# Modulation rows by blocks of 512 columns, with two tiles of x modulated ahead of the scale

## The chip, the cores and the metric

The kernel runs on one NeuronCore of a Trainium2 chip. The metric is the device time of one execution in microseconds, taken as the median of a few executions of the same program. Five engines work side by side, each through its own instructions in program order: TensorE (PE, matrix products into the eight PSUM banks of 128 x 512 words), VectorE (DVE), ScalarE (ACT), GpSimd (POOL) and SyncE (SP, which here only issues DMA). They wait for each other by semaphores.

## The reference, cut to what matters

One batch of 2048 rows (S) of 1024 columns (D). All six modulation rows come from one vector `c`.

```python
mod = (_silu(c) @ w_mod).reshape(c.shape[0], 6, 1, -1)
sa, ca, ga, sb, cb, gb = ...                       # six rows of 1024
h = _layernorm(x) * (1 + ca) + sa
x = x + ga * fourier(h)        # real part of a DFT along D, then along S, by products
h = _layernorm(x) * (1 + cb) + sb
x = x + gb * (gelu(h @ w1 + b1) @ w2 + b2)         # 1024 -> 3584 -> 1024
```

The change concerns the first line, for `sa` and `ca` (the first 2048 columns of `w_mod`, 8 MB), and the first use of them: `h` for the first two of the sixteen tiles of 128 rows of x.

## The kernel before, in words

Every large product is made in half precision from split operands. A value is written as a high half (an f16 copy, by ScalarE) and a low half (the rest, by VectorE), and each product is three passes: high by high, high by low, low by high. So every operand costs ScalarE one instruction and VectorE one before TensorE can use it.

The Fourier part comes first. `plain1` (its products are line 1121) makes the first block of 512 output columns of the DFT along S by sixteen operands n of 48 products each: n = 0 to 7 use the real half of the DFT matrix, and each brings in a new pair of tiles of x, k and k + 8; n = 8 to 15 use the imaginary half with the same x. `winograd1` (line 1171) makes the other three blocks with fewer products from combined quarters; `gemm2` (line 1403) is the DFT along D; `gemm3` and `gemm4` (lines 1597 and 1706) are the two layers of the MLP.

A tile of x passes through `x_tasks`. Its mean and square sum are made by ScalarE (lines 610 and 614, each with an accumulated sum) or, for the first pair, by VectorE's statistics (601, 603); a few VectorE steps on 128 x 2 values turn them into the factor of the row (623 to 627). Then VectorE subtracts the mean and multiplies by the row 1 + ca (642), multiplies by the factor and adds the row sa (643); ScalarE takes the high half (644), VectorE the low half (645), and `("h", k, n)` is ready. `split_c` (690, 693) does the same for the two halves of an operand of the DFT matrix, with 690 on ScalarE and 693 on VectorE.

The rows sa and ca must first be scaled by a power of two from their largest value, so that they fit f16. Before, the 8 MB come as eight loads of one k each (128 partitions x 2048 columns, 8 KB in one run); `mod_pe` sums k = 0, 3, 5 and 7 on TensorE in four banks with a copy of silu(c) as the left operand, in single precision (each such product of 512 columns is two passes in the trace); `mod_dve` sums k = 1, 2, 4 and 6 on VectorE in `macc`, one instruction over 2048 columns for each. Four products with ones (line 1474) add `macc` to the banks over the partitions, and `mod_rows` adds k = 7 (496), takes the maximum of each bank (516), makes the scale `sh` (517 to 520), modulates tile 0 in two halves (503, 508, 521, 526, 513), and writes the rows `sas` and `ca1s` out of PSUM for the other tiles (521, 527, 528). The second tile of the pair, tile 8, follows like every other.

The order of all work is written out when the program is built. The start, up to `mod_rows`, is written by hand; from there a planner holds a model clock for every engine (`clk`), a time at which each result is done (`done`), and streams of tasks with due times (`push`). Between the products of TensorE, `fill_to` emits the task that is due first among those that could start. `clk.update(...)`, `done["mod"]`, `done["h", 0, 0]` behind the hand-written part set the model's state, and `LANDS` how long a stored piece takes until it may be loaded again (`("st", "u")`: the pieces of the first DFT's result). Due times come from `T0 = 42.0` and 48 products of 0.2158 us for each n. So the hand-written part also settles the order that VectorE, ScalarE, GpSimd and SyncE have later.

Of the kernel before, what the change touches and what calls it, by code (L numbers as in the profile page):

```python
# [17 lines left out]
P = 128  # L18
# [17 lines left out]
def kernel(ctx, tc, x, cre, cim, dre, dim, w1, b1, w2, b2, c, wm, out):  # L36
# [180 lines left out]
    LANDS = {"dma": 2.0, "st": 4.0, ("st", "d"): 7.0, ("st", "u"): 5.0, ("st", "s"): 4.0, ("st", "z"): 4.0}  # L217
# [253 lines left out]
    def wm2(k):  # L471

        return at(O_U + 8 * k if k < 4 else O_H + 8 * (k - 4), 2048)

    def mbank(n):
        return banks8[:, 512 * n : 512 * n + 512]

    def mod_pe(k, first):

        for n in range(4):  # L480
            if first and n > 1:
                pe.matmul(mbank(n), ones[0:1, 0:P], ones[0:1, :], start=True, stop=False)
            pe.matmul(mbank(n), srep[:, k, :], wm2(k)[:, 512 * n : 512 * n + 512], start=first and n < 2, stop=False)

    def mod_dve(k, first):

        if first:
            dve.tensor_scalar(macc, wm2(k), scol[:, k : k + 1], None, op0=ALU.mult)
        else:
            dve.scalar_tensor_tensor(macc, wm2(k), scol[:, k : k + 1], macc, op0=ALU.mult, op1=ALU.add)  # L490

    def mod_rows(k, c_lo, x1):


        for n in (2, 3, 0, 1):
            pe.matmul(mbank(n), srep[:, k, :], wm2(k)[:, 512 * n : 512 * n + 512], start=False, stop=True)
        m, pm, sh, iu = (m1[:, j : j + 1] for j in range(4))
        (mv, cl), x_ = xs[0], xf(0)
        r, a = cl[:, 1, :], cl[:, 2, :]
        sl = [slice(512 * q, 512 * q + 512) for q in range(2)]  # L500

        def times_ca(q):
            dve.scalar_tensor_tensor(
                x_[:, sl[q]], x_[:, sl[q]], mv[:, 0, 0:1], mbank(2 + q), op0=ALU.subtract, op1=ALU.mult
            )

        def plus_sa(q):
            dve.scalar_tensor_tensor(
                x_[:, sl[q]], x_[:, sl[q]], r[:, 0:1], sas[:, sl[q]], op0=ALU.mult, op1=ALU.add
            )  # L510

        def lo(q):
            dve.tensor_tensor(hq[:, 3 * q, 0, 1], x_[:, sl[q]], hq[:, 3 * q, 0, 0], op=ALU.subtract)

        for j in (2, 3, 0, 1):
            dve.tensor_reduce(mx[:, j : j + 1], mbank(j), axis=AX.X, op=ALU.max, apply_absolute_value=True)
        dve.tensor_reduce(m, mx, axis=AX.X, op=ALU.max)
        pow2(pm, m)
        dve.reciprocal(sh, pm)
        dve.tensor_scalar(sh, sh, SH, None, op0=ALU.mult)  # L520
        act.activation(sas[:, sl[0]], mbank(0), AF.Copy, scale=sh)
        times_ca(0)
        dve.scalar_tensor_tensor(r, r, sh, a, op0=ALU.mult, op1=ALU.mult)
        plus_sa(0)
        x1.pop(0).run()
        act.activation(hq[:, 0, 0, 0], x_[:, sl[0]], AF.Copy)  # L526
        act.activation(sas[:, sl[1]], mbank(1), AF.Copy, scale=sh)
        act.activation(ca1s, banks8[:, 1024:2048], AF.Copy)
        x1.pop(0).run()
        c_lo.run()  # L530
        lo(0)
        times_ca(1)
        plus_sa(1)
        act.activation(hq[:, 3, 0, 0], x_[:, sl[1]], AF.Copy)
        x1.pop(0).run()
        lo(1)
        dve.tensor_scalar(iu, pm, 2.0**5 / SD, None, op0=ALU.mult)

# [49 lines left out]
    xst = [mk([P, 2, 12], F32, f"xst{n}") for n in range(2)]  # L588
    xs = [(mk([P, 2, 2], F32, f"xmv{n}"), mk([P, 4, 2], F32, f"xcl{n}")) for n in range(8)]

    def x_tasks(k):

        st, (mv, cl) = xst[k % 2], xs[k]
# [3 lines left out]
        if k < 1:  # L597
            for n, i in enumerate(tiles):
                sv = st[:, n].rearrange("p (h k) -> p h k", h=2)
                for h in range(2):  # L600
                    f = lambda sv=sv, h=h, i=i: dve.bn_stats(sv[:, h], xf(i)[:, 512 * h : 512 * h + 512])
                    t.append(Task("dve", 0.7, f, [("x", i)] + ([t[-1].key] if t else [])))
                t.append(Task("dve", 0.2, lambda sv=sv, n=n: dve.bn_aggr(mv[:, n], sv), [t[-1].key]))
            t += chain(("dve", 0.15, lambda: dve.tensor_scalar(ve, mv[:, :, 1], EPS, None, op0=ALU.add)))
            t[-1].deps = (t[-2].key,)
        else:

            junk = at(O_U, 1024, F16)
            for n, i in enumerate(tiles):
                f = lambda n=n, i=i: act.activation(junk, xf(i), AF.Copy, accum_out=mv[:, n, 0:1])  # L610
                t.append(Task("act", 1.35, f, [("x", i)]))
            t.append(Task("dve", 0.15, lambda: dve.tensor_scalar(ss, mv[:, :, 0], -1.0 / D, None, op0=ALU.mult), [t[-1].key]))
            for n, i in enumerate(tiles):
                f = lambda n=n, i=i: act.activation(junk, xf(i), AF.Square, bias=ss[:, n : n + 1], accum_out=mv[:, n, 1:2])
                t.append(Task("act", 1.35, f, [t[2].key]))

            def var():
                dve.tensor_scalar(ve, mv[:, :, 1], 1.0 / D, EPS, op0=ALU.mult, op1=ALU.add)

            t.append(Task("dve", 0.15, var, [t[-1].key]))  # L620
# [10 lines left out]
        if k == 0:  # L631
            s.pop()
        t += s
        root = t[-1].key
        for n, i in enumerate(tiles):
            if i == 0:
                continue
            x_, hv = xf(i), hq[:, 1:3, k] if n else hq[:, 0:4:3, k]
            x2 = x_.rearrange("p (q d) -> p q d", q=2)
            mean, op = (mv[:, n, 0:1], ALU.subtract) if k < 1 else (ss[:, n : n + 1], ALU.add)  # L640
            u = chain(
                ("dve", 1.3, lambda x_=x_, mean=mean, op=op: dve.scalar_tensor_tensor(x_, x_, mean, ca1s, op0=op, op1=ALU.mult)),  # L642
# [792 lines left out]
    def load_wm2(k):  # L1435
        sp.dma_start(wm2(k), wm[:, k, 0 : 2 * D])

# [16 lines left out]
    for k in range(7):  # L1454
        if k in (1, 2, 4, 6):
            mod_dve(k, k == 1)
        else:
            mod_pe(k, k == 0)
# [9 lines left out]
    done["x", 0] = done["x", 8] = 23.0  # L1468
    clk.update(dma=45.0, act=15.0, dve=22.0, pe=25.0)
    x0 = x_tasks(0)  # L1470
    for _ in range(12):
        x0.pop(0).run()
    for n in (2, 3, 0, 1):
        pe.matmul(mbank(n), ones[:, 0:P], macc[:, 512 * n : 512 * n + 512], start=False, stop=False)
# [519 lines left out]
```

## Time and profile before

| | |
|---|---|
| median of 3 runs | 1980.11 us (1979.96 to 1980.17) |
| profiled execution | 1977.33 us |
| its span, first to last instruction | 1975.6 us |
| mean granted TensorE clock | 0.997 |
| PE busy | 1950.2 us (99%) |
| DVE busy | 1426.9 us (72%) |
| ACT busy | 851.2 us (43%) |
| read and written in HBM | 263 MB and 138 MB |

How to read it. A line of the timeline gives the start, the time from start to end of the merged instructions, the engine, the line of the kernel, what is written and read with its shape, how many instructions were merged, and in brackets the idle time of the engine before it with what released it. A line of the windows gives a stretch, its length, the busy time and number of instructions of PE, the weight loads, DVE, ACT and POOL, then the granted TensorE clock (1.00 is full speed), the share of the DMA engines, and GB/s. A line of waits gives who waited, for whom, the sum, the number and the longest. PE's busy time counts a product from its start to its modelled end, and consecutive products overlap; their spacing is found from a run of them.

### The profile page before, as it was taken

The numbers are of one execution on the slowest core, as the hardware profiler recorded it, in microseconds if no ns is written. First come the engines' busy times: TensorE is split into PE (matmuls) and PEld (weight loads), VectorE is DVE, ScalarE is ACT, GpSimd is POOL, SyncE is SP. The second block draws the span as 40 slices with busy tenths as digits, with TensorE's granted clock in tenths as the row PEclk, the third lists the DMA queues.
The fourth block names the chain that finished last, engine by engine and source line by source line (L and its number), as shares of the span: only waits on it lengthen the run. The fifth ranks groups of instructions, "written<-read, shape, count | busy, mean of one in ns | idle before, by whom it ended". The sixth has DMA issues, their size and how long they took to land.

```text
span 1975.6 us, 23586 instructions
## 1 busy us (share of the span) xinstructions
PE 1950.2 (99%) x9004; PEld 887.3 (45%) x9004; DVE 1426.9 (72%) x1799; ACT 851.2 (43%) x1091; POOL 190.3 (10%) x282
## 2 busy tenths in 40 slices
PE   7999999999999999999999999999999999999999
PEld 2444444444444444444444444444444444444443
DVE  5977886898984477776689898989873453553566
ACT  4743432445542255554587456456323312312311
POOL 0012211221210012211020000000000000000000
PEclk9999999999999999999999999999999999999999
DMA  9248587688688867878866455344476432432324
GB/s 386 61 165 271 187 287 292 236 324 314 241 280 328 308 236 254 288 234 302 309 221 204 142 181 176 134 148 176 176 218 197 124 102 74 131 102 66 112 75 85
DMA packets 139362, 402.41 MB, mean 204 GB/s; under 512 B 15536, under 2 KB 15536, under 8 KB 134640
## 3 DMA queue, kind: packets, MB, share of 16 engines
q1 hardware_dynamic: 112528, 309.92, 46.6%
q0 software_dynamic: 26720, 90.98, 13.0%
q8 instruction: 70, 1.15, 0.2%
q14 instruction: 44, 0.36, 0.0%
HBM read 262.95 MB, written 137.89 MB: 203 GB/s over the span
## 4 chain that ended last, share of the span: by engine, by line
PE 84%; DVE 8%; DMA 4%; ACT 2%; issue 1%; SPq 0%; DVEq 0%; ACTq 0%
PE ps L1706 24%; PE ps L1597 24%; PE ps L1171 17%; PE ps L1403 14%; PE ps L1121 5%; DMA arena<-in_wm_dram 2%; DVE arena L693 1%; DMA arena<-s 1%; DVE arena L642 1%; DVE arena L407 1%; DVE arena L643 1%; DMA arena<-u 1%; PE ps L1305 1%; DVE arena L645 1%; DVE arena L553 1%
## 5 line engine op out<-in xcount | busy, mean ns | idle before, releaser
L1706 PE MATMUL ps<-arena 128*128 128x512 f16 x2352 | 511.2, 379 | 2.7 <-DMA arena<-w 1.1
L1597 PE MATMUL ps<-arena 128*128 128x512 f16 x2352 | 510.2, 379 | 0.0
L1171 PE MATMUL ps<-arena 128*128 128x512 f16 x2016 | 435.6, 379 | 1.8 <-DMA arena<-s 1.8
L1706 PEld LDWEIGHTS <-arena 128*128 128x128 f16 x2352 | 229.9, 98 | 281.8 <-issue 3.9
L1597 PEld LDWEIGHTS <-arena 128*128 128x128 f16 x2352 | 230.2, 98 | 276.8
L1752 DVE SCALAR_TENSOR_TENSOR arena<-ps,i4c,arena 128x1024 f32<-128x1024 f32 x179 | 229.3, 1281 | 145.2 <-PE ps L1706 143.1
L1171 PEld LDWEIGHTS <-arena 128*128 128x128 f16 x2016 | 197.1, 98 | 240.2 <-DMA arena<-s 2.8
L1403 PE MATMUL ps<-arena 128*128 128x512 f16 x1344 | 292.4, 379 | 0.9 <-DMA arena<-u 0.9
L395 ACT ACTIVATE arena<-arena,shc 128x512 f16<-128x512 f32 (+1 forms) x115 | 116.2, 1018 | 283.2 <-PE ps L1706 190.4
L1403 PEld LDWEIGHTS <-arena 128*128 128x128 f16 x1344 | 131.4, 98 | 157.1 <-DMA arena<-u 1.4
L1121 PE MATMUL ps<-arena 128*128 128x512 f16 x768 | 171.3, 386 | 7.0 <-ACT arena L526 3.9
L420 DVE TENSOR_TENSOR arena<-arena 128x512 f32<-128x512 f32 (+1 forms) x228 | 171.1, 753 | 4.2
L690 ACT ACTIVATE arena<-arena 128x1024 f16<-128x1024 f32 x100 | 104.1, 1050 | 146.9 <-PE ps L1171 113.1
L407 DVE SCALAR_TENSOR_TENSOR arena<-arena,shc 128x512 f16<-128x512 f32 (+1 forms) x115 | 128.5, 1121 | 35.8 <-ACT arena L395 35.4
L693 DVE SCALAR_TENSOR_TENSOR arena<-arena 128x1024 f16<-128x1024 f32 x100 | 128.6, 1303 | 18.6 <-ACT arena L690 18.6
L1623 DVE TENSOR_TENSOR arena<-arena,ps 128x512 f32<-128x512 f32 x84 | 57.6, 685 | 111.2 <-PE ps L1597 106.9
L1616 ACT ACTIVATE arena<-arena,b1s,i1c 128x512 f32<-128x512 f32 x84 | 68.3, 813 | 137.7 <-DVE arena L1623 137.7
L1121 PEld LDWEIGHTS <-arena 128*128 128x128 f16 x768 | 75.8, 99 | 102.8 <-issue 8.8
L782 ACT ACTIVATE arena<-arena 128x1024 f16<-128x1024 f32 x56 | 57.8, 1048 | 62.0 <-DMA u<-arena 21.4
L395 ACT ACTIVATE arena<-arena,s1c 128x512 f16<-128x512 f32 (+1 forms) x70 | 60.7, 884 | 41.3 <-DVE arena L420 30.1
L785 DVE TENSOR_TENSOR arena<-arena 128x1024 f16<-128x1024 f32 x56 | 66.9, 1218 | 15.0 <-ACT arena L782 15.0
L407 DVE SCALAR_TENSOR_TENSOR arena<-arena,s1c 128x512 f16<-128x512 f32 (+1 forms) x70 | 66.1, 959 | 10.8 <-ACT arena L395 10.7
(161 smaller groups left out, 1392.6 us busy)
## 6 DMA issues: line engine op xcount, KB each, us to landing
w<-arena SPq DMA_DIRECT2D x64, 512.0 KB, 4.3
arena<-w SPq DMA_DIRECT2D x119, 256.0 KB, 2.7
u<-arena POOLq DMA_DIRECT2D x56, 512.0 KB, 5.4
arena<-u SPq DMA_DIRECT2D x112, 256.0 KB, 4.2
arena<-w SPq DMA_DIRECT2D x56, 512.0 KB, 3.6
arena<-s SPq DMA_DIRECT2D x48, 512.0 KB, 7.7
arena<-in_cre_dram SPq DMA_DIRECT2D x32, 512.0 KB, 7.1
arena<-in_cim_dram SPq DMA_DIRECT2D x32, 512.0 KB, 5.6
```

Of the source, the lines that this page charges most:

```text
L395: act.activation(o[m][0], q(j), AF.Copy, **sc)
L407: dve.scalar_tensor_tensor(o[m][1], q(j), scale, o[m][0], op0=ALU.mult, op1=ALU.subtract)
L420: dve.tensor_tensor(q(d), q(a), q(b), op=op)
L690: h = Task("act", 1.15, lambda: act.activation(o[:, :, 0], s2, AF.Copy, scale=SC), list(deps) + free)
L693: dve.scalar_tensor_tensor(o[:, :, 1], s2, SC, o[:, :, 0], op0=ALU.mult, op1=ALU.subtract)
L1121: pe.matmul(bank_of(d_), hleft(d_, s, kp, a), cop(n)[:, s, b], start=(kp == 0 and s == 0 and a == 0 and b == 0), stop=(kp == 7 and s == 1 ...
L1171: pe.matmul(bank_of(st + ch), left, cop(n)[:, s, b], start=(start and kp == 0 and s == 0 and a == 0 and b == 0), stop=(kp == 3 and s == 1 ...
L1403: pe.matmul(bank_of(bk), up(N)[:, c_, a], dp(n)[:, c_, w], start=(start and ri == 0 and c_ == 0 and i == 0), stop=(ri == 1 and c_ == 3 and ...
L1597: pe.matmul(ps.rearrange("p (k t) -> p k t", k=4), w1c[:, m, s, a, d * P : (d + 1) * P], zc(m)[:, b, :, d, :], start=(start and d == 0 and ...
L1616: act.activation(dst, src, AF.Gelu_apprx_tanh, scale=inv, bias=b1s[:, 2 * p + j : 2 * p + j + 1])
L1706: pe.matmul(t[:, j], hidc[:, c_, m, a, k * P : (k + 1) * P], w2c[:, m, c_, w], start=(start and c_ == 0 and n == 0), stop=(c_ == 1 and n = ...
L1752: lambda: dve.scalar_tensor_tensor(dst, ps[b], inv, dst, op0=ALU.mult, op1=ALU.add), kp[b],
```

## The change

- The weights of the four half rows are loaded by column blocks of 512 in the order `MODS = (2, 0, 3, 1)`: first half of ca, first half of sa, second half of ca, second half of sa. A load has four k (128 x 4 x 512, runs of 2 KB); the last block's second load is cut into two of two k. Tiles 0 and 8 of x are loaded behind the first block.
- The sums lie in the last four banks instead of the first four. Within each block some k are summed by TensorE (`mod_pe`) and some by VectorE (`mod_dve`, now 512 columns at a time); `mod_sum` adds VectorE's part, `mod_top` takes the maximum of a bank as soon as it is complete.
- Tiles 0 and 8 get their mean and variance from ScalarE, and ScalarE makes `(x - mean) * factor` of both with one instruction each (`AF.Identity`). Tile 0's halves are multiplied by ca and sa is added straight from PSUM, and tile 8 is multiplied by ca, before the scale is known. With the scale, ScalarE's high half of tile 0 applies it in the same instruction, the low half likewise on VectorE; tile 8 takes one VectorE step with the scaled row `sas`. Tile 0 itself is multiplied by the scale at the end of the part.
- Tile 9's statistics move from ScalarE to VectorE.
- Fourteen products of a constant tile that nobody reads stand at the start of TensorE's order, and eight behind the last sum (`idle_pe`).
- The planner's starting state differs (`pe` 29.5 instead of 34.0, `("h", 0, 0)` 29.5 instead of 35.0, `("h", 0, 1)` given as 35.0, `mod` 33.5 instead of 33.0), and a stored u counts as landed after 7 instead of 5 us.

```diff
-    LANDS = {"dma": 2.0, "st": 4.0, ("st", "d"): 7.0, ("st", "u"): 5.0, ("st", "s"): 4.0, ("st", "z"): 4.0}
+    LANDS = {"dma": 2.0, "st": 4.0, ("st", "d"): 7.0, ("st", "u"): 7.0, ("st", "s"): 4.0, ("st", "z"): 4.0}
...
+    def load_wmb(n, k, w):
+        sp.dma_start(wmb(n, k, w), wm[:, k : k + w, 512 * n : 512 * n + 512])
+
+    def idle_pe(n):
+        w = ones.bitcast(F16)
+        for _ in range(n):
+            pe.matmul(banks8[:, 0:512], w[:, 0:P], w[:, 0:512], start=True, stop=True)
+
+    def mod_pe(n, k, first=False):
+        if first and n > 1:
+            pe.matmul(mbank(n), ones[0:1, 0:P], ones[0:1, :], start=True, stop=False)
+        pe.matmul(mbank(n), srep[:, k, :], wmb(n, k)[:, 0], start=first and n < 2, stop=False)
...
+    def mod_sum(n):
+        pe.matmul(mbank(n), ones[:, 0:P], acc_of(n), start=False, stop=True)
+
+    def mod_top(n):
+        dve.tensor_reduce(mx[:, n : n + 1], mbank(n), axis=AX.X, op=ALU.max, apply_absolute_value=True)
...
-    load_wm2(0)
-    for k in range(1, 7):
-        load_wm2(k)
-    for i in (0, 8):
-        load_x(i).run()
-    load_wm2(7)
+    for n in MODS:
+        for k, w in ((0, 4), (4, 4)) if n != 1 else ((0, 4), (4, 2), (6, 2)):
+            load_wmb(n, k, w)
+        if n == 2:
+            load_x(0).run()
+            load_x(8).run()
...
+    idle_pe(14)
+    part(2, (0, 1, 2, 3), 2, True)
+    part(2, (4, 5, 6, 7), 3)
+    steps("act", "act", "dve", "act", "act")
+    part(0, (0, 1, 2, 3), 2, True)
+    mod_sum(2)
+    steps("dve", "act")
+    part(0, (4, 5, 6, 7), 3)
+    steps("dve", "dve", "dve", "dve")
+    dve.tensor_tensor(r, r, a, op=ALU.mult)
+
+    dve.tensor_tensor(ss, ss, r, op=ALU.mult)
+    for n, v in enumerate((x_, y_)):
+        act.activation(v, v, AF.Identity, scale=r[:, n : n + 1], bias=ss[:, n : n + 1])
+    mod_top(2)
+    part(3, (0, 1, 2, 3), 2, True)
+    mod_sum(0)
+    dve.tensor_tensor(xh[0], xh[0], mbank(2), op=ALU.mult)
+    part(3, (4, 5, 6, 7), 3)
+    dve.tensor_tensor(xh[0], xh[0], mbank(0), op=ALU.add)
+    mod_top(0)
+    part(1, (0, 1, 2, 3), 2, True)
+    mod_sum(3)
+    mod_top(3)
+    part(1, (4, 5), 1)
+    dve.tensor_tensor(xh[1], xh[1], mbank(3), op=ALU.mult)
+    part(1, (6, 7), 1)
+    mod_sum(1)
+    idle_pe(8)
     c_hi, c_lo = c0[0][1]
     c_hi.run()
+    dve.tensor_tensor(y_, y_, both(2), op=ALU.mult)
+    mod_top(1)
+    dve.tensor_reduce(m, mx, axis=AX.X, op=ALU.max)
+    pow2(pm, m)
+    dve.reciprocal(sh, pm)
+    dve.tensor_scalar(sh, sh, SH, None, op0=ALU.mult)
+    act.activation(hq[:, 0, 0, 0], xh[0], AF.Copy, scale=sh)
+    dve.tensor_tensor(xh[1], xh[1], mbank(1), op=ALU.add)
+    act.activation(hq[:, 3, 0, 0], xh[1], AF.Copy, scale=sh)
+    dve.scalar_tensor_tensor(hq[:, 0, 0, 1], xh[0], sh, hq[:, 0, 0, 0], op0=ALU.mult, op1=ALU.subtract)
+    act.activation(sas, both(0), AF.Copy, scale=sh)
+    c_lo.run()
+    dve.scalar_tensor_tensor(hq[:, 3, 0, 1], xh[1], sh, hq[:, 3, 0, 0], op0=ALU.mult, op1=ALU.subtract)
+    act.activation(ca1s, both(2), AF.Copy)
     x1 = x_tasks(1)
-    for _ in range(2):
+    x1.pop(0).run()
+
+    y2, hv = y_.rearrange("p (q d) -> p q d", q=2), hq[:, 1:3, 0]
+    dve.scalar_tensor_tensor(y_, y_, sh, sas, op0=ALU.mult, op1=ALU.add)
+    act.activation(hv[:, :, 0], y2, AF.Copy)
+    x1.pop(0).run()
+    x1.pop(0).run()
+    dve.tensor_tensor(hv[:, :, 1], y2, hv[:, :, 0], op=ALU.subtract)
+    for _ in range(6):
         x1.pop(0).run()
-    mod_rows(7, c_lo, x1)
-    clk.update(act=34.0, dve=35.0, pe=34.0)
-    done["mod"] = 33.0
-    done["h", 0, 0] = 35.0
-    push("x0", "x", x0, 20.0)
+    dve.tensor_scalar(x_, x_, sh, None, op0=ALU.mult)
+    dve.tensor_scalar(iu, pm, 2.0**5 / SD, None, op0=ALU.mult)
+    clk.update(act=33.5, dve=35.0, pe=29.5)
+    done["mod"] = 33.5
+    done["h", 0, 0] = 29.5
+    done["h", 0, 1] = 35.0
```

`part(n, ks, of_pe)` hands the first `of_pe` of the k in `ks` to `mod_pe` and the rest to `mod_dve`; `steps` emits the next tasks of tile pair 0; `both(n)` is two neighbouring banks.

More of the change, by code (lines that the diff above doesn't have):

```diff
@@ L492, in mod_rows @@
[L492 to L537, printed above, removed]
@@ L596, in x_tasks @@
         t = []
[L597 to L620, printed above, removed]
@@ L1467 @@
             c0[k][0].run()
-    done["x", 0] = done["x", 8] = 23.0
-    clk.update(dma=45.0, act=15.0, dve=22.0, pe=25.0)
-    x0 = x_tasks(0)
[L1471 to L1474, printed above, removed]
+    done["x", 0] = done["x", 8] = 12.0
+    clk.update(dma=45.0, act=12.0, dve=12.0, pe=25.0)
+    m, pm, sh, iu = (m1[:, j : j + 1] for j in range(4))
+    (mv, cl), x_, y_ = xs[0], xf(0), xf(8)
@@ new lines, with part, steps @@
+    r, a, ss = (cl[:, j] for j in (1, 2, 3))
+    xh = [x_[:, 512 * q : 512 * q + 512] for q in range(2)]
+    x0 = x_tasks(0)
+    idle_pe(14)
+    def part(n, ks, of_pe, first=False):
+        for k in ks[:of_pe]:
+            mod_pe(n, k, first and k == 0)
+        for k in ks[of_pe:]:
+            mod_dve(n, k, first and k == ks[of_pe])
+    def steps(*engines):
+        for e in engines:
+            t = x0.pop(0)
+            assert t.eng == e
+            t.run()
+    part(2, (0, 1, 2, 3), 2, True)
```

68 lines of the change are left out of this document (44 added, 24 removed).

## The prediction

> **What bounds the kernel now.** I read the page first, then TensorE's waits, TensorE's timeline, the chain that ended last, and the windows with the granted clock.
>
> ```profile
> span 1975.6 us, 23586 instructions
> PE 1950.2 (99%) x9004; PEld 887.3 (45%) x9004; DVE 1426.9 (72%) x1799; ACT 851.2 (43%) x1091; POOL 190.3 (10%) x282
> ```
>
> ```profile
> PE ps L1121 <- ACT arena L526: 3.9, 1, 3.9
> PE ps L1171 <- DMA arena<-s: 1.8, 2, 0.9
> ...
> PE ps L1403 <- DMA arena<-u: 0.9, 1, 0.9
> PE ps L1706 <- DMA arena<-w: 1.1, 1, 1.1
> ```
>
> TensorE is busy for 1950.2 of 1975.6 us, so an edit at the start can win only part of the 25 us it is not. After the first stage its waits are single ones of about 1 us. The room is in the first 120 us:
>
> ```profile
> 6.86 3.75 PE L483 MATMUL ps<-arena 128*128 128x512 f32 x4 [6.86 <-DMA arena<-in_wm_dram]
> ...
> 19.32 3.70 PE L483 MATMUL ps<-arena 128*128 128x512 f32 x8 [0.68 <-DMA arena<-in_wm_dram]
> ...
> 27.80 3.60 PE L496 MATMUL ps<-arena 128*128 128x512 f32 x8
> ```
>
> ```profile
> 35.25 1.16 PE L1121 MATMUL ps<-arena 128*128 128x512 f16 x2 [3.86 <-ACT arena L526]
> ...
> 37.52 12.10 PE L1121 MATMUL ps<-arena 128*128 128x512 f16 x45 [0.20 <-DVE arena L503]
> 51.09 0.38 PE L1121 MATMUL ps<-arena 128*128 128x512 f16 x1 [1.46 <-ACT arena L690]
> 52.53 72.75 PE L1121 MATMUL ps<-arena 128*128 128x512 f16 x328 [1.07 <-DVE arena L693]
> ```
>
> ```profile
> 41.00:42.00 1.00, 1.00 (x4) 0.33 (x3) 1.00 (x1) 0.97 (x3) 0.00 (x0) 0.50 1.02 406
> 42.00:43.00 1.00, 1.00 (x6) 0.40 (x5) 0.46 (x3) 1.00 (x3) 0.00 (x0) 0.97 0.99 393
> ...
> 52.00:53.00 1.00, 0.47 (x2) 0.19 (x2) 1.00 (x2) 0.97 (x3) 0.00 (x0) 0.65 0.00 0
> ...
> 55.00:56.00 1.00, 1.00 (x4) 0.40 (x3) 1.00 (x2) 0.97 (x2) 0.00 (x0) 0.64 0.85 328
> ```
>
> ```profile
> 60.00:117.00 57.00, 57.00 (x266) 25.75 (x264) 54.25 (x77) 35.32 (x51) 1.27 (x1) 1.00 0.22 65
> ```
>
> ```profile
> 116.08 1.21 DVE arena L645
> 117.34 91.99 PE ps L1121 x426
> ```
>
> The reader is to see three things. The products start at 35.25 after a wait of 3.86 us, run at half clock (0.50 granted) until 42, catch up with their operands, wait 1.46 and 1.07 us, and lose clock again (0.65 granted at 52, 0.64 at 55). From 52.53 to 125 TensorE does not wait: 328 products in 72.75 us. But VectorE is busy for 54.25 of the 57 us from 60 to 117, and the chain passes from it to TensorE at 117.3: the second low half of the last x tile (L645) ends at 117.29 and TensorE uses it at 117.34. Both engines come in together there. So the end moves with the later of the two at this place, and a gain for TensorE before it counts only as far as VectorE follows.
>
> **The change part by part.** Rows for the prices (the first two are DMA of 0 to 30 and 28 to 50 us, the rest single instructions):
>
> ```profile
> q1 hardware_dynamic: 2248, 11.23, 93.7%
> ```
>
> ```profile
> q1 hardware_dynamic: 2902, 8.82, 102.4%
> ```
>
> ```profile
> L1623 DVE TENSOR_TENSOR arena<-arena,ps 128x512 f32<-128x512 f32 x84 | 57.6, 685 | 111.2 <-PE ps L1597 106.9
> ```
>
> ```profile
> 1.18 3.80 SPq L1436 DMA_DIRECT2D arena<-in_wm_dram  x7
> ...
> 9.31 1.29 DVE L488 TENSOR_SCALAR arena<-arena,scol 128x2048 f32<-128x2048 f32 x1 [7.87 <-DMA arena<-in_wm_dram]
> ...
> 24.12 1.28 DVE L601 BATCH_NORM_STATS2 xst<-arena 128x6 f32<-128x512 f32 x2
> ...
> 31.43 0.69 DVE L516 TENSOR_REDUCE mx<-ps 128x1 f32<-128x512 f32 x1 [0.17 <-PE ps L496]
> ...
> 32.73 0.15 DVE L520 TENSOR_SCALAR m<-m 128x1 f32<-128x1 f32 x1
> ...
> 33.78 0.75 DVE L508 SCALAR_TENSOR_TENSOR arena<-arena,xcl 128x512 f32<-128x512 f32 x1
> ...
> 34.56 0.63 ACT L526 ACTIVATE arena<-arena 128x512 f16<-128x512 f32 x1 [0.96 <-DVE arena L508]
> ...
> 35.67 1.02 ACT L528 ACTIVATE arena<-ps 128x1024 f32<-128x1024 f32 x1
> ...
> 43.39 1.23 DVE L645 TENSOR_TENSOR arena<-arena 128x1024 f16<-128x1024 f32 x1 [0.78 <-ACT arena L644]
> ```
>
> ```profile
> 49.03 1.06 ACT L644 ACTIVATE arena<-arena 128x1024 f16<-128x1024 f32 x1 [0.51 <-DVE arena L643]
> ```
>
> ```profile
> 50.12 1.23 DVE L645 TENSOR_TENSOR arena<-arena 128x1024 f16<-128x1024 f32 x1 [0.52 <-ACT arena L644]
> 51.26 1.22 DVE L693 SCALAR_TENSOR_TENSOR arena<-arena 128x1024 f16<-128x1024 f32 x1
> ...
> 54.98 1.28 DVE L642 SCALAR_TENSOR_TENSOR arena<-arena,xcl 128x1024 f32<-128x1024 f32 x1
> ...
> 59.72 1.22 DVE L645 TENSOR_TENSOR arena<-arena 128x1024 f16<-128x1024 f32 x1
> ```
>
> *Loads.* The same 8 MB of modulation weights come, in runs of 2 KB where before 8 KB, with tiles 0 and 8 after the first 2 MB instead of after the seventh. Before, five loads lie between 6.86 and 19.32: 2.49 us each. The queue moved 11.23 MB in 28.1 us of full share (0.40 MB/us) with the large runs, 8.82 in 22.5 (0.39) with runs of 2 and 4 KB; I take 2.6 us a load. Landings: column block 2 at 6.9 and 9.5, tiles 10.8 and 12.0, block 0 at 14.6 and 17.2, block 3 at 19.8 and 22.4, block 1 at 25.0, 26.3 and 27.6. SyncE issues one more load for the weights, in its own time: its seven first took 3.80 us, 0.54 each. The x and cre loads behind come 0.7 us later than before, and wait in their buffers anyway.
>
> *TensorE up to the scale.* Eight passes take 3.43 us (3.60 less the drain), so one f32 product of 512 columns costs 0.857. From block 0 on there are 14 weight products, 4 sums and one product of ones, 19 x 0.857 = 16.3 us, back to back: sum of block 2 at 17.2, of block 0 at 23.2, of block 3 at 28.4, the last two weight products at 30.1. The 14 unused products at the start lie before the first load; the 8 behind the last sum (1.7 us at full clock) end before the first real product.
>
> *VectorE up to the scale.* In its order the maximum of bank 3 stands ahead of the last two shares of block 1. It waits for the sum at 28.55, and behind it queue 0.69, a share 0.75, a product from PSUM 0.685, the last share 0.75 (overlaps of 0.08 taken off): 31.2. TensorE waits for that share; its last sum ends at 32.1, visible 32.3; maximum to 33.0, and from there the same four small steps as before (0.76): the scale is known at 33.75. Before it was at 32.88 (L520). So the scale comes 0.9 us *later*. Bounds: 33.3 with loads at 2.49, 35.5 if the wait of 2.5 us ahead of block 0 (12.1 to 14.6) halves the clock for a window, as the two of 1.46 and 1.07 did.
>
> *After the scale.* Tile 0 needs only one ScalarE copy (0.63): first product 34.45, 0.8 us earlier than 35.25, at full clock. VectorE then does one addition, two low halves, L693 and tile 8's single step; ScalarE writes both rows (2 x 1.02) and tile 8's high half: tile 8 is complete at 40.65, before at 44.62. Now the statistics that were done early before are still due: two halves of tile 9 (1.28), four small steps, the scaling of tile 0 (0.65 by half of L488), the root's five. Tile 1's two products begin at 44.35, its low half ends at 49.2 (before 51.35), and L693 of the second operand at 50.35 (52.48). TensorE, done with its first 48 products by 46, waits about 4 us, loses a window of clock as before, and is 2.15 us ahead.
>
> *Where it goes.* VectorE loses this again. Before, L642 of tile 2 filled the wait for ScalarE at 54.98, its root being ready; now tile 2's and tile 3's roots are still to do (5 steps of about 0.2 each), and 0.95, 0.3 and 0.65 us pass in waits for L644. Adding the steps in the changed order: 50.35, tile 9's products and low half to 55.25, root 56.2, L693 57.35, tile 2's products to 60.45, its low half after ScalarE to 62.75. Before that low half ended at 60.94. From there on the two orders differ by four small steps (0.8 us) that have already been done; the tail from L656 is the same. So the last low half comes 62.75 - 60.94 - 0.8 = 1.0 us later, at 118.3. Bounds of this term: -2.15 (all of the lead kept) and +3 (the clock lost ahead of block 0).
>
> *The clock there.* TensorE could be at this place at about 115, so it waits some 3 us where it did not wait before. The waits of 1.46 and 1.07 gave the dip of 52 to 55; a single one of 0.9 later keeps the clock at 1.00:
>
> ```profile
> 302.00:304.00 2.00, 1.09 (x6) 0.31 (x4) 0.00 (x0) 1.05 (x1) 0.00 (x0) 1.00 0.99 385
> ```
>
> By the 0.65 and the 0.64 at its two ends the dip lasted 0.7 + 2 + 0.7 = 3.4 us at half clock, so 1.7 us is lost if all falls on products, nothing if the wait splits over several tiles. I take +1.0, nearer the upper end, which is the row like it. The Trainium skill (TensorE: Matmul & The Clock Gate, Part 1: The HAM clock gate) has fixed windows of 3413 ns and says the clock drops after at least one idle window; by that rule a wait of 3 us costs nothing and the sum would be 1.0 us smaller. The trace agrees on the length of the window, but dropped the clock at 52.5 after a shorter total wait.
>
> *Behind 125 us.* Nothing is computed differently. But the planner starts from other clocks and takes 7 instead of 5 us for a stored u to land, so VectorE's, ScalarE's and the queues' orders between about 230 and 1000 us are different (TensorE's is the same but for its transposes). SyncE's queue has loads of s, u and w that TensorE waited for by 0.9 to 1.1 us each. Bounds: -2.8 if those four waits go, +5 if a few loads of 512 KB (1.3 us each) come behind others. I take 0.
>
> Sum: +1.0 + 1.0 + 0 = +2.0 us. The profiled execution took 1977.33 us, 1.7 outside its span; the runs' median is 1980.11, and I add to that: **1982.1**.
>
> **The rivals.** *The lead survives* (faster): VectorE fills its waits, the last x tile is no bound, and the 2.15 us at the second operand reach the end; 1978.0, or 1975.2 if the later waits go too. For it: ScalarE is busy only 35 of 57 us there. Against: VectorE's 54.25 of 57. *A queue order costs* (slower): the loads of s or u come late at 303 us or a later such place, where the DMA share is 0.99 already; from two 512 KB transfers on it decides; with four, 5.2 us on top of the 1.0: 1986. For it: three of TensorE's four later waits are of DMA, at that same margin. *The clock holds* as the rule has it: 1981.1. *The unused products do not do what they say*: at half clock behind 34.45 TensorE loses 3.4 us that its wait of 4 us at 46 swallows; no time of its own.
>
> **How the numbers follow.** Forecast 0.40, clock holds 0.10, lead survives 0.22, queue order 0.28. About 0.2% (4.0 us) is what a measurement can tell. Faster by more: 0.13, the part of the second case with the later waits gone. Slower by more: 0.23 of the last case and 0.04 of the first. The rest, 0.60, is within. The likeliest case by its bounds reaches from 1979 to 1985; with both others, 1975.0 to 1988.0.
>
> **What would show it.** Scale at 33 to 35 and first product near 34.5 at clock 1.00; L645 of tile 1 near 49; a wait of TensorE of 2 to 4 us for L645 near 115, with clock 0.50 behind it. The forecast is wrong if that wait is missing and the products of the first stage end before 209.3 (117.34 + 91.99), or if the waits for s, u or w grow beyond 2 us each.

## The result, and the profile after

The changed kernel takes 1984.72 us (median of 6 runs, 1984.06 to 1988.68), the kernel before 1978.68 on the same chip (6 runs, 1976.92 to 1980.17): ratio 1.0038 (1.0028 to 1.0048), so 0.4% slower. The profiled execution took 1984.97 us with a span of 1983.2, 7.6 more than before. Runs of one and the same kernel lie 3.3 us (before) and 4.6 us (after) apart here, and up to 7.9 in a series below (e7), so what follows argues from stage times inside the traces first and from medians second.

The page's first lines and TensorE's waits, of the changed kernel (who waited, for whom; sum, number, longest):

```profile
span 1983.2 us, 23674 instructions
...
PE 1959.7 (99%) x9032; PEld 891.1 (45%) x9032; DVE 1426.1 (72%) x1810; ACT 855.1 (43%) x1096; POOL 188.2 (9%) x282
```

```profile
PE ps L499 <- DMA arena<-in_wm_dram: 3.0, 2, 2.2
PE ps L1153 <- DVE arena L675: 2.7, 1, 2.7
PE ps L1103 <- ACT arena L672: 2.7, 1, 2.7
PE ps L1103 <- ACT arena L626: 2.2, 1, 2.2
...
PE ps L509 <- DVE arena L506: 1.0, 1, 1.0
...
PE ps L1103 <- DVE arena L627: 0.7, 1, 0.7
...
PE ps L1153 <- DMA arena<-s: 0.2, 1, 0.2
```

L499 and L509 are `mod_pe` and `mod_sum`, L506 `mod_dve`; L624 to L627 are the steps of a tile of x that were 642 to 645, L672 and L675 the halves of an operand (690 and 693), L1103 and L1153 the products of `plain1` and `winograd1`. Two waits are new: 2.2 + 0.7 us for the last x tile (L626, L627), and 2.7 us for an L675 in `winograd1`, where before it was 0.9 for a DMA. TensorE's timeline places them (start, us, merged products, the wait in brackets):

```profile
8.71 6.36 PE L499 MATMUL ps<-arena 128*128 128x512 f32 x10 [0.89 <-DMA arena<-in_wm_dram]
17.22 1.98 PE L499 MATMUL ps<-arena 128*128 128x512 f32 x4 [2.15 <-DMA arena<-in_wm_dram]
...
34.45 1.13 PE L509 MATMUL ps<-arena 128*128 128x512 f32 x2 [0.98 <-DVE arena L506]
...
38.02 1.04 PE L1103 MATMUL ps<-arena 128*128 128x512 f16 x4 [0.72 <-ACT arena L1500]
...
52.29 0.38 PE L1103 MATMUL ps<-arena 128*128 128x512 f16 x1 [2.69 <-ACT arena L672]
53.74 64.56 PE L1103 MATMUL ps<-arena 128*128 128x512 f16 x290 [1.07 <-DVE arena L675]
120.50 0.60 PE L1103 MATMUL ps<-arena 128*128 128x512 f16 x2 [2.21 <-ACT arena L626]
121.77 13.51 PE L1103 MATMUL ps<-arena 128*128 128x512 f16 x54 [0.67 <-DVE arena L627]
...
431.44 224.37 PE L1153 MATMUL ps<-arena 128*128 128x512 f16 x1031 [2.71 <-DVE arena L675]
```

VectorE's timeline gives the scale (L1499, known at 36.92 + 0.15 = 37.07 us; before at 32.88) and the last low half (L627, ends at 121.72; before at 117.28):

```profile
31.78 0.69 DVE L512 TENSOR_REDUCE mx<-ps 128x1 f32<-128x512 f32 x1 [2.47 <-PE ps L509]
...
36.92 0.15 DVE L1499 TENSOR_SCALAR m<-m 128x1 f32<-128x1 f32 x1
...
42.92 1.23 DVE L1516 TENSOR_TENSOR arena<-arena 128x1024 f16<-128x1024 f32 x1 [1.11 <-ACT arena L1513]
...
64.83 1.22 DVE L627 TENSOR_TENSOR arena<-arena 128x1024 f16<-128x1024 f32 x1 [0.59 <-ACT arena L626]
...
120.50 1.22 DVE L627 TENSOR_TENSOR arena<-arena 128x1024 f16<-128x1024 f32 x1
```

The windows of the loads, of the changed kernel and then of the one before (the last two numbers are the share of the DMA engines and GB/s):

```profile
2.00:9.00 7.00, 6.11 (x17) 2.14 (x16) 0.32 (x1) 2.85 (x6) 0.00 (x0) 1.00 0.94 277
9.00:27.00 18.00, 15.85 (x32) 5.90 (x31) 8.43 (x20) 7.36 (x11) 0.28 (x1) 0.91 1.04 390
```

```profile
2.00:9.00 7.00, 2.14 (x3) 1.14 (x4) 0.00 (x0) 2.85 (x6) 0.00 (x0) 1.00 0.97 357
9.00:27.00 18.00, 16.08 (x33) 5.68 (x33) 11.06 (x10) 0.00 (x0) 1.05 (x1) 1.00 1.01 419
```

The DMA engines are as busy after as before, but move 277 instead of 357 GB/s up to 9 us, and 390 instead of 419 behind: 7 x 80 + 18 x 29 = 1080, so 1.1 MB less by 27 us, or 2.8 us at 390 GB/s. The first block, at 8.71 us, is 1.8 us late already against the 6.9 of the prediction.

The table has the stage times of all kernels run. "Scale" is the end of the last small step of the scale, "low half" the end of the last x tile's low half, "s" the start of TensorE's run behind its wait near 424 us, "last" the start of the last run of 127 products, all in us from the start of the span. Each row is one profiled execution.

| kernel | scale | low half | low half - scale | s | s - low half | last |
|---|---|---|---|---|---|---|
| before | 32.88 | 117.28 | 84.40 | 424.06 | 306.78 | 1943.53 |
| after | 37.07 | 121.72 | 84.65 | 431.44 | 309.72 | 1951.21 |
| e1 runs of 8 KB | 35.40 | 120.08 | 84.68 | 429.89 | 309.81 | 1949.36 |
| e2 no unused products | 36.64 | 121.32 | 84.68 | 430.54 | 309.22 | 1949.87 |
| e3 shares first | 36.93 | 121.61 | 84.68 | 432.19 | 310.58 | 1951.20 |
| e4 before + unused products | 35.75 | 120.17 | 84.42 | 426.26 | 306.09 | 1945.35 |
| e5 after, order of before | 36.75 | 120.47 | 83.72 | 427.45 | 306.98 | 1946.91 |
| e6 before + two low halves | 33.11 | 120.03 | 86.92 | 428.94 | 308.91 | 1948.23 |
| e7 before, u lands at 7 | 32.79 | 117.20 | 84.41 | no wait | | 1942.64 |
| e8 all mended | 32.43 | 116.45 | 84.02 | 421.89 | 305.44 | 1940.96 |
| e9 tile 9 on ScalarE | 34.78 | 117.50 | 82.72 | 423.48 | 305.98 | 1943.22 |
| e10 as e9, runs of 2 KB | 35.71 | 118.40 | 82.69 | 425.48 | 307.08 | 1944.55 |
| e11 e8 without its statistics | 34.64 | 118.39 | 83.75 | 425.78 | 307.39 | 1945.43 |
| e12 e9 again | 34.38 | 117.07 | 82.69 | 423.53 | 306.46 | 1942.28 |

### The profile page after: what moved, and what is told of

Same layout as the page of the kernel before. It is cut to its first block, busy times and chain, and to the rows that moved or that the text cites. A ratio compares the mean times of both kernels' runs of the same rounds, so it can differ in the third digit from the quotient of the medians.

```text
span 1983.2 us, 23674 instructions
## 1 busy us (share of the span) xinstructions
PE 1959.7 (99%) x9032; PEld 891.1 (45%) x9032; DVE 1426.1 (72%) x1810; ACT 855.1 (43%) x1096; POOL 188.2 (9%) x282
## 4 chain that ended last, share of the span: by engine, by line
PE 82%; DVE 10%; DMA 3%; issue 2%; ACT 2%; SPq 0%; DVEq 0%; ACTq 0%
PE ps L1746 24%; PE ps L1637 24%; PE ps L1385 15%; PE ps L1153 14%; PE ps L1103 5%; DMA arena<-in_wm_dram 3%; DVE arena L675 2%; DVE arena L407 1%; DVE arena L624 1%; DVE arena L625 1%; DVE arena L707 1%; PE ps L1287 1%; DVE arena L627 1%; DVE arena L528 1%; DVE arena L767 1%
## 5 line engine op out<-in xcount | busy, mean ns | idle before, releaser
L1153 PE MATMUL ps<-arena 128*128 128x512 f16 x2016 | 437.3, 380 | 2.9 <-DVE arena L675 2.7
L1153 PEld LDWEIGHTS <-arena 128*128 128x128 f16 x2016 | 197.6, 98 | 242.4 <-issue 5.3
L1103 PE MATMUL ps<-arena 128*128 128x512 f16 x768 | 170.2, 384 | 8.3 <-ACT arena L672 2.7
L672 ACT ACTIVATE arena<-arena 128x1024 f16<-128x1024 f32 x100 | 103.9, 1049 | 149.0 <-PE ps L1153 111.2
L675 DVE SCALAR_TENSOR_TENSOR arena<-arena 128x1024 f16<-128x1024 f32 x100 | 128.6, 1302 | 27.9 <-ACT arena L672 27.6
L1103 PEld LDWEIGHTS <-arena 128*128 128x128 f16 x768 | 75.7, 99 | 102.8 <-issue 7.7
L1659 ACT ACTIVATE arena<-ps 128x512 f32<-128x512 f32 x84 | 49.6, 591 | 55.2 <-PE ps L1637 55.1
```

The source lines that it names most:

```text
L672: h = Task("act", 1.15, lambda: act.activation(o[:, :, 0], s2, AF.Copy, scale=SC), list(deps) + free)
L675: dve.scalar_tensor_tensor(o[:, :, 1], s2, SC, o[:, :, 0], op0=ALU.mult, op1=ALU.subtract)
L1103: pe.matmul(bank_of(d_), hleft(d_, s, kp, a), cop(n)[:, s, b], start=(kp == 0 and s == 0 and a == 0 and b == 0), stop=(kp == 7 and s == 1 ...
L1153: pe.matmul(bank_of(st + ch), left, cop(n)[:, s, b], start=(start and kp == 0 and s == 0 and a == 0 and b == 0), stop=(kp == 3 and s == 1 ...
```

## The experiments

**e1, loads in runs of 8 KB.** The first 2048 columns of the weights are handed over a second time, laid out by blocks of 512 columns, so that a load of four k is one run of 8 KB for each partition.

```diff
-        sp.dma_start(wmb(n, k, w), wm[:, k : k + w, 512 * n : 512 * n + 512])
+        sp.dma_start(wmb(n, k, w), wmm[:, n, k : k + w, :])
```

> The changed kernel, with the weights of sa and ca laid out by column block in the input, so that each load is one run of 8 KB (the last two 4 KB) a partition instead of 2 KB; nothing else differs. Theory A (the short runs made the scale late, and VectorE's chain from the scale to the last x tile carries that to the end): first block lands near 6.9 us instead of 8.7, the scale at 33.5 to 34.5 instead of 37.1, the last low half of x (L627) near 119 instead of 122.4, the whole 2.5 to 4 us faster than the changed kernel, that is 3 to 5 us slower than before. Rival B (the loads are hidden, the loss is made behind 60 us by the new orders): the scale may move, the whole changes by less than 1 us.

1983.11 us (7 runs) against 1977.74 for the kernel before (18 runs): 1.0025 (1.0014 to 1.0036). Its windows:

```profile
2.00:9.00 7.00, 7.00 (x21) 2.42 (x19) 1.26 (x3) 2.85 (x6) 0.00 (x0) 1.00 0.94 359
9.00:27.00 18.00, 15.78 (x32) 6.35 (x33) 9.23 (x21) 7.35 (x11) 0.32 (x1) 0.91 1.02 417
```

359 and 417 GB/s, as before: the length of the runs sets the rate, at a DMA share that looks the same. The Trainium skill (Perfetto Trace Analysis, DMA Optimizations) advises to batch small transfers into larger ones, 2 KB into 4 or 8 KB; it does not speak of the runs within one load of 1 MB, but these windows go the same way, 277 against 359. But the scale comes only 1.67 us earlier, because TensorE's clock fell in this run behind a wait (its timeline: four passes take 3.33 us at 13.99, against 1.98 in the changed kernel at 17.22):

```profile
13.99 3.33 PE L499 MATMUL ps<-arena 128*128 128x512 f32 x4 [2.22 <-DMA arena<-in_wmm_dram]
...
118.87 0.60 PE L1103 MATMUL ps<-arena 128*128 128x512 f16 x2 [2.23 <-ACT arena L626]
```

From the scale on nothing changes: the same wait for the last x tile, 84.68 us from the scale to its low half. The last run of products starts 1.85 us earlier, so what the scale gained reaches the end as theory A has it, but not its 2.5 to 4 us; in the times the two kernels are not told apart (1.0025 against 1.0038, with intervals that overlap).

**e2, no unused products.**

```diff
-    idle_pe(14)
...
-    idle_pe(8)
```

> The changed kernel without its 14 + 8 unused products. Theory A: the first products are at half clock up to about 45 us, TensorE waits less at 49 us, and the end does not move (within 1 us). Rival B (TensorE's own pace in the first stage decides): 2 to 4 us slower than the changed kernel. A third reading, that the 14 products at the start slow the first loads: the first block lands near 7 us instead of 8.7 and the scale comes 1.5 us earlier.

1984.96 us (5 runs), 1.004 (1.0028 to 1.0053). The first 48 products run at half clock in part and take 12.29 us, TensorE waits 1.99 instead of 2.69 us for the second operand, and from the scale to the last low half it is 84.68 us again. The products do raise the clock and win nothing; they do not slow the first load by much either (8.34 against 8.71 us, and 8.34 again in e10, which has them).

**e3, shares first.** VectorE's last shares of block 1 stand ahead of the maximum of bank 3.

```diff
-    mod_top(3)
     part(1, (4, 5), 1)
-    dve.tensor_tensor(xh[1], xh[1], mbank(3), op=ALU.mult)
     part(1, (6, 7), 1)
+    mod_top(3)
     mod_sum(1)
+    dve.tensor_tensor(xh[1], xh[1], mbank(3), op=ALU.mult)
```

> The changed kernel with VectorE's last two shares (k = 5 and k = 7 of block 1) ahead of the maximum of bank 3, so that they do not wait for that bank's sum. Theory A: TensorE's last sum no longer waits for VectorE (0.98 us), the scale comes 0.7 to 1.3 us earlier, and the whole is faster than the changed kernel by as much. Rival B: less than 0.5 us.

1984.19 us (6 runs), 1.0031 (1.002 to 1.0043). The last sum follows without its wait of 0.98 us, but the clock fell at 16.77 us in this run (four passes took 3.57 us), and the scale stands at 36.93. The price of the queue is read better between the changed kernel and e10, which has the shares first, the same runs of 2 KB and, like the changed kernel, a full clock from 17 us on: 37.07 - 35.71 = 1.36 us, of which 0.11 was there when the second block of columns was taken up (17.22 and 17.11), so 1.25.

**e4, unused products in the kernel before.** Fourteen of them behind its last modulation sum.

```diff
+        w = ones.bitcast(F16)
+        for _ in range(14):
+            pe.matmul(banks8[:, 2048:2560], w[:, 0:P], w[:, 0:512], start=True, stop=True)
```

> The kernel before with 14 unused products behind the last sum of the modulation rows, and nothing else. Theory A: the first 48 products run at full clock and end near 46 us instead of 49.6, TensorE then waits some 4 us for the second operand, and the end does not move: within 1 us of before. Rival B (half clock at the start costs): 2 to 3.5 us faster than before.

1978.07 us (11 runs), 1.0000 (0.9991 to 1.0009). A warm clock at the first products (21 of them in 4.69 us at 40.39) is worth nothing, since the last x tile is bound by VectorE: TensorE waits 0.80 + 0.67 us for it, and from the scale it is 84.42 us, as before. The profiled run is not a clean copy, though. Its row stage was slow ahead of the unused products (at 12 to 16 us two passes take 2.07 us, 1.12 in the kernel before), so that the scale stands 2.87 us later, and the wait of 4 us at the second operand came as 1.20 + 0.65 at tile 8 and 1.49 + 1.07 there.

**e5, the later order of before.**

```diff
-    ("st", "u"): 7.0
+    ("st", "u"): 5.0
...
-    clk.update(act=33.5, dve=35.0, pe=29.5)
-    done["mod"] = 33.5
-    done["h", 0, 0] = 29.5
+    clk.update(act=38.0, dve=39.0, pe=36.0)
+    done["mod"] = 33.0
+    done["h", 0, 0] = 35.0
```

> The changed kernel with the planner started so that VectorE, ScalarE, GpSimd and SyncE have the order of the kernel before from the second stage on: a stored u lands after 5 instead of 7, and the clocks start at act 38, dve 39, pe 36 with mod at 33 and both first halves of h at 35. Theory A, the new order costs by itself: the wait of 2.71 us for L675 near 431 us falls back to about 0.9 for DMA, and the end comes about 2 us earlier, 1982.5. Theory B, that wait follows from everything being later by 5 us: it stays between 2 and 4, and the time stays at 1984.5. The last x tile of the first stage should stay near 120 to 122 us in both, since the start is not touched.

1980.85 us (11 runs) against 1977.25 (32 runs): 1.0019 (1.001 to 1.0027), so about half of the loss. The wait near 431 is gone, replaced by one for a DMA as before (first VectorE's timeline in the changed kernel, with the instructions ahead of the late operand; then TensorE's in e5):

```profile
426.70 1.22 DVE L707 TENSOR_TENSOR arena<-arena 128x1024 f32<-128x1024 f32 x1
427.84 1.22 DVE L815 SCALAR_TENSOR_TENSOR arena<-arena 128x1024 f16<-128x1024 f32 x1
428.97 0.68 DVE L832 TENSOR_TENSOR arena<-arena 128x512 f32<-128x512 f32 x1
429.57 0.68 DVE L833 TENSOR_TENSOR arena<-arena 128x512 f32<-128x512 f32 x1
430.18 1.21 DVE L675 SCALAR_TENSOR_TENSOR arena<-arena 128x1024 f16<-128x1024 f32 x1
```

```profile
427.45 222.91 PE L1153 MATMUL ps<-arena 128*128 128x512 f16 x1032 [1.21 <-DMA arena<-s]
```

The late operand is the 58th L675 of the trace, in e2 and e3 as well. In the kernel before (its L693) the 58th ended at 414.33, nearly 10 us ahead of the products at 424.06, as the second of this pair:

```profile
411.98 2.35 DVE L693 SCALAR_TENSOR_TENSOR arena<-arena 128x1024 f16<-128x1024 f32 x2
```

In e5 it ended at 417.57. Theory A stands: the stretch "s - low half" is 306.98 us, as before's 306.78, against 309.22 to 310.58 in the four kernels with the new order. I had also expected the first stage to stay as it was. It did not: the planner's clocks settle VectorE's order there too, and 83.72 instead of 84.65 us pass from the scale to the last low half.

**e6, two more low halves in the kernel before** (those of pair 6 are taken twice, 2 x 1.14 us).

```diff
-    dve.tensor_tensor(hv[:, :, 1], x2, hv[:, :, 0], op=ALU.subtract)
+    [dve.tensor_tensor(hv[:, :, 1], x2, hv[:, :, 0], op=ALU.subtract) for _ in range(2 if k == 6 else 1)]
```

> The kernel before, with VectorE taking the two low halves of tile pair 6 twice (2 x 1.14 us more on VectorE near 100 to 106 us; output unchanged). Theory A, VectorE's chain bounds the last x tile: TensorE waits 1.5 to 2.3 us near 117 for the last low half and the end comes as much later, 1979.3 to 1980.0, up to 1.7 more if the clock loses a window there. Theory B, TensorE has slack at that place: no wait, 1977.7.

1982.03 us (10 runs), 1.0022 (1.0013 to 1.0032).

```profile
118.82 0.60 PE L1121 MATMUL ps<-arena 128*128 128x512 f16 x2 [3.21 <-ACT arena L644]
120.09 15.22 PE L1121 MATMUL ps<-arena 128*128 128x512 f16 x62 [0.67 <-DVE arena L645]
```

The stretch from the scale grows by 86.92 - 84.40 = 2.5 us, TensorE now waits, and the last run of products starts 4.7 us later: 2.75 at the last tile, 0.23 of which was there at the scale, and 2 behind it, 1.7 of that by the clock (94.00 us for the rest of the stage against 92.33, see below). Theory A holds. This is the cost of the changed kernel's first stage, made in the kernel before with one line.

**e7, a stored u lands at 7 in the kernel before.**

```diff
-    ("st", "u"): 5.0
+    ("st", "u"): 7.0
```

> The kernel before with only the planner's figure for a stored u at 7 instead of 5. Theory A, that figure's order costs: a wait of TensorE near 424 us or behind it grows to 2 to 3 us, 1979 to 1980. Theory B, it is the planner's other start that moved the operand near 431, and the figure is free: the waits stay at 0.7 to 1.1, 1977.7.

1977.62 us (11 runs), 1.0006 (0.9997 to 1.0015): theory B, the figure alone costs nothing that can be measured. That leaves the planner's start as the cause of e5's gain; in the changed kernel the two were not run apart.

**e8, all mended.** e1's loads, VectorE's order of e3, e5's start (dve at 38), and ScalarE's sum of tile 1 ahead of the scale and those of tiles 2 and 10 behind tile 8.

```diff
     c_hi.run()
+    x1 = x_tasks(1)
+    x1.pop(0).run()
...
     act.activation(hv[:, :, 0], y2, AF.Copy)
+    x2 = x_tasks(2)
+    x2.pop(0).run()
+    x2.pop(0).run()
     dve.tensor_tensor(hv[:, :, 1], y2, hv[:, :, 0], op=ALU.subtract)
```

> The changed kernel with loads in runs of 8 KB, the last shares ahead of the maximum of bank 3, ScalarE's sum of tile 1 ahead of the scale and those of tiles 2 and 10 behind tile 8, and the later order of the kernel before. Theory A, the four causes are the loads, the queue ahead of the scale, the statistics still due and the order: scale at 34 to 35, last low half of the x tiles at 116 to 119, wait near 424 at 0.9, time 1977 to 1980. Theory B, VectorE's lead is lost by something else: last low half at 120 or later, 1981 or more.

1977.4 us (11 runs), 1.0002 (0.9993 to 1.0011): the whole loss is gone. In the profiled run the clock held through the row stage, and the scale is known at 32.43 us, 0.45 earlier than before. Against e10, whose clock also held, runs of 8 KB are worth 35.71 - 32.43 = 3.28 us at the scale. The two differ in other things too; e9 and e10, which differ by the loads alone, take up the second block at 14.62 and 17.11 us, so 2.5 to 3.3 us is what the runs show. Much of it can be lost again: with 8 KB the clock fell at this block in e1, e9, e11 and e12 and held in e8 alone, with 2 KB it fell there in e3 alone.

**e9, tile 9 back on ScalarE**, its first sum ahead of the scale, and tile 0's scaling in a wait of VectorE; the planner starts with act at 40 and dve at 39. **e10** is e9 with the loads of the changed kernel (e1's edit undone), **e11** is e8 without the early sums of the diff above (and with dve at 39, as in e5), **e12** is e9 again.

```diff
-        own = (0,) if k == 1 else (0, 1)
+        own = (0, 1)
...
+    x1.pop(0).run()
     x1.pop(0).run()
     both = lambda n: banks8[:, 2048 + 512 * n : 3072 + 512 * n]
...
+    x1.pop(0).run()
+    dve.tensor_scalar(x_, x_, sh, None, op0=ALU.mult)
     dve.tensor_tensor(hv[:, :, 1], y2, hv[:, :, 0], op=ALU.subtract)
```

> As e8, with the statistics of tile 9 back on ScalarE (both sums of pair 1 ahead of the scale, where ScalarE waits for 2.13 us) and the scaling of tile 0 in VectorE's wait for tile 8's high half; planner started so that the later order is the one of before. Theory A, VectorE's steps and waits between the scale and 60 us carry the last x tile: tile 1's products begin about 2 us earlier (43.10 in e8), no wait at the last x tile near 116, the end 1 to 2 us ahead of e8, 1975.5 to 1976.5. Theory B, from e8 on the end is set by other things: 1977.4 within a us.

> As e9, with the weights in their old place in memory and runs of 2 KB. Theory A, the loads cost 1.6 to 1.85 us at the scale, and TensorE's lead at the last x tile swallows none of it since VectorE's chain is close behind: 1.5 us above e9. Theory B, the start has slack by now: equal to e9.

> The changed kernel with the loads in runs of 8 KB, the last shares ahead of the maximum of bank 3 and the planner's start of e5, but the statistics left where the change put them (e8 without its third part). Theory A, statistics still due cost VectorE's lead: last low half of the x tiles 1 to 2 us later than in e8 (there it was used at 116.5) and the end 1 us later, 1978.5. Theory B, loads, shares and order explain all: as e8, 1977.4.

> The kernel of e9 once more, on whichever chip comes. If its lead of 0.11% is real: 0.998 to 0.9995 again, and the last low half of the x tiles near 115.5 to 117.5 us with TensorE waiting less than 1 us for it. If it was scatter: 0.9995 to 1.0005.

| | median us (11 runs each) | before | ratio |
|---|---|---|---|
| e9 | 1975.56 | 1978.44 | 0.9989 (0.998 to 0.9998) |
| e10 | 1977.99 | 1978.44 | 0.9995 (0.9986 to 1.0004) |
| e11 | 1976.85 | 1978.44 | 0.9989 (0.998 to 0.9998) |
| e12 | 1974.75 | 1977.63 | 0.999 (0.9981 to 0.9999) |

e9 is faster than both kernels, by 0.1% against the kernel before, twice; e11 reaches the same ratio, once, so the times do not tell these two apart. e9 needs the weights in their other layout, and e10 without it is not told apart from the kernel before. Its gain stands where theory A put it, in the stretch from the scale to the last low half (82.72 and 82.69 against 84.02), though not as I had it: VectorE's first product for tile 1 begins 10.03 us behind the scale, 10.67 in e8, so 0.6 earlier and not 2. In e11 theory A fails: without e8's early sums that stretch is 83.75 us, no longer than with them, and it is not slower than e8. So e8's early sums won nothing; e9's 1.3 us came with taking tile 9's statistics off VectorE and with the scaling in a wait, and these two were not run apart. e10 against e9: 0.93 us at the scale, 0.90 at the last low half, 1.3 at the last run of products, though e9's clock fell in its row stage (four passes in 3.60 us) and e10's did not.

## Why the prediction was right and wrong

The time fell into the range (1984.72 in 1975.0 to 1988.0) and on the side of the forecast, slower. But it is 0.38% and not 0.1%: beyond the 0.2% within which I had put the likeliest case. Against the kernel before on the same chip it is 6.0 us where I had 2.0; the forecast looks nearer because it was added to a median of 1980.11, 1.4 above the 1978.68 measured here. That it still lies within 1979 to 1985, the bounds of my likeliest case, is luck in part: 2.9 us of it came behind 125 us, where I took 0. Of the signs named, the wait at the last x tile came (2.21 + 0.67 us, with clock 0.50 behind it) and the waits for s, u and w stayed short, but the scale (37.07, not 33 to 35) and the first product (38.02, not near 34.5) did not come when they should.

*What bounds the kernel: right.* From the scale to the last low half VectorE's chain takes 84.65 to 84.68 us in four kernels with the same order, whatever the loads and TensorE's clock do (after, e1, e2, e3), and 84.40 to 84.42 in three with the order of before (before, e4, e7). e4 and e6 show it from both sides: a gain for TensorE counts nothing, 2.28 us more on VectorE lengthen the stretch by 2.52.

*The steps behind the scale: right.* Counted from the scale, which I had at 33.75: tile 8 complete 6.90 predicted, 44.15 - 37.07 = 7.08 measured; tile 2's low half 29.00, measured 64.83 + 1.22 - 37.07 = 28.98; last low half 84.55, measured 84.65. The lead is lost where I said: here are the windows from 50 to 60 us, of the kernel before and of the changed one (VectorE is the third pair).

```profile
50.00:60.00 10.00, 7.84 (x29) 3.30 (x30) 9.85 (x11) 9.07 (x15) 0.00 (x0) 0.83 0.21 68
```

```profile
50.00:60.00 10.00, 6.64 (x23) 2.73 (x24) 7.73 (x14) 9.40 (x16) 0.00 (x0) 0.83 0.51 175
```

It is busy 7.73 instead of 9.85 us. At the same distance from the scale, 45.81 to 55.81 us, the kernel before has 9.02, so the fair difference is 1.29 us. The waits that I had at 0.95, 0.3 and 0.65 us are 0.98, 0.27 and 0.59, the first and the last of them for ScalarE's high halves.

*The loads: the first step that failed.* The scale came 4.19 us later, where I took 0.9 and bounded it by 35.5. The landing times were wrong. I had the first block at 6.9 and the second (block 0) at 14.6; they were used at 8.71 and 17.22, and this 2.6 us is most of the 3.3 between 33.75 and 37.07. The other 0.7 lies between that block and the scale. The rate of my row, 0.39 MB/us from 28 to 50 us, is what the loads had behind 9 us (390 GB/s), but up to 9 us they had 277. With the clock held, runs of 2 KB cost up to 3.28 us at the scale (e10 to e8). The queue on VectorE, which I had seen and priced in, costs 1.25 to 1.36. By the stages of e10 and e8, 3.28 + 1.36 - 0.45 = 4.19: without the two the new row stage is 0.45 us ahead of the old one, as e8 shows. I also had SyncE's issues at 0.54 us each; the seven loads behind the x tiles took 16.87, and 7.34 in e1 with its runs of 8 KB:

```profile
3.60 16.87 SPq L487 DMA_DIRECT2D arena<-in_wm_dram  x7
```

*The clock at the last x tile: right in size at its place, but not a term of the sum.* The chain of waits has 94.02 us for the products from there to the end of the stage, and 92.33 in e3, where the same wait left the clock alone:

```profile
121.77 94.02 PE ps L1103 x427
```

```profile
121.66 92.33 PE ps L1103 x427
```

So 1.7 us, the upper bound that I gave. Yet the kernels that kept the clock are not earlier near 431 us: e3 waits there 4.07 and e2 3.49 us for L675, after 2.71. VectorE reaches that operand no sooner, and the wait takes back what the clock did not lose.

*Behind 125 us: the second step that failed.* I took 0, and for the rival a load that comes late. The waits for s, u and w shrank or stayed (0.91 became 0.17 near 303). What came late was a product operand of VectorE, the 58th L675, behind work that the planner had put ahead of it, the last four instructions of which are shown under e5: "s - low half" is 2.94 us longer than before, 2.74 of which is gone in e5. The rival of 1986 came near the measured 1984.72 by luck: it had 5.2 us in loads that come late, the order cost 2.9, and the place and the engine were others. One bound was added up wrongly: the four waits of DMA that the prediction shows are 1.8 + 0.9 + 1.1 = 3.8 us, not 2.8, so the best case would have been 1974.2; nothing measured here hangs on it.

The sum as measured: 4.19 at the scale, 0.25 on VectorE's way to the last tile, 2.94 up to the wait near 431 (the clock's 1.7 within it), 0.30 behind: 7.68 us at the last run of products.

*The other rivals.* The lead did not survive. That the clock holds was so in e2 and e3 and not in the changed kernel, e1 and e6. The unused products did as they say behind the last sum and had no time of their own (e2, e4).

## What to carry to other kernels

Find the value that everything later hangs on (here the scale) and measure from it: if the stretch behind it is constant to 0.03 us between kernels, as here in four, then what comes before it reaches the end of that stretch in full; the stretch itself shrank where work was taken off its engine (1.3 us in e9). The finer split of the loads was paid for with shorter runs, and the price failed because its row came from another part of the kernel. And a planner's start state is part of a change: in e5 clocks set 4 to 6.5 us later, with the old figure for u, took a wait of 2.7 us away 400 us behind the start.

## What the runs showed of the hardware that was not expected

- Loads in runs of 2 KB moved 277 GB/s up to 9 us and 390 behind, at a DMA share of 0.94 and 1.04; runs of 8 KB 359 and 417 at 0.94 and 1.02. The share does not tell the two apart.
- The granted clock of the page can read 1.00 where TensorE is slow. In e4 it is 1.00 throughout, yet two passes in single precision take 2.07 us at 12.39 and 14.39 us, and eight take 3.60 at 27.23.
- TensorE's clock does not follow the length of a wait. At the last x tile the same 2.2 + 0.7 us cost a stretch of half clock in the changed kernel and in e1 and none in e2 and e3; in the row stage it fell behind waits of 2.22 (e1), 2.21 (e9, e11) and 2.49 us (e3) and not behind 2.15 (after, which had a stretch of 0.50 just ahead, behind a wait of 0.89) and 2.66 us (e10). The windows of the changed kernel show one such stretch (the granted clock is third from the end):

```profile
121.00:122.00 1.00, 0.34 (x2) 0.13 (x2) 1.00 (x2) 0.40 (x1) 0.00 (x0) 0.90 0.17 12
122.00:123.00 1.00, 1.00 (x3) 0.30 (x2) 1.00 (x2) 0.52 (x1) 0.00 (x0) 0.50 0.68 145
...
124.00:125.00 1.00, 1.00 (x4) 0.34 (x3) 0.00 (x0) 0.02 (x1) 0.00 (x0) 0.50 0.17 27
125.00:126.00 1.00, 1.00 (x5) 0.42 (x4) 0.00 (x0) 0.58 (x1) 0.00 (x0) 0.90 0.71 215
```

  0.2 + 3 + 0.2 = 3.4 us. The Trainium skill (TensorE: Matmul & The Clock Gate, Part 1: The HAM clock gate) states windows of that length that run free of the kernel, and a drop after at least one idle one. The length agrees; a drop after 2.9 us of waiting does not, and whether a window's place decides between e1 and e2, no run here shows.
